# A scan and a gated feed-forward block on one core: unit 1's running states added by VectorE, in a new instruction order

## The chip, the cores and the metric

The kernel runs on one core of a Trainium2 chip. TensorE multiplies, VectorE, ScalarE and GpSimd work on elements, and SyncE's queue issues most transfers. In the profile they are PE (and PEld for its weight loads), DVE, ACT, POOL and SP. The metric is the device time of one execution in microseconds (us); less is better.

## The reference, cut to what matters

```python
# B, H, S, D = 4, 8, 768, 48
mag = sqrt(a_re**2 + a_im**2)
scale = minimum(mag, 0.999) / (mag + 1e-6)
for t in range(S):                       # per batch and head, S_re and S_im are D x D
    S_re, S_im = ar*S_re - ai*S_im + outer(k[t], v[t]), ar*S_im + ai*S_re
    y[t] = q[t] @ S_re                   # ar, ai: a_re, a_im times scale, by row of the state
x = y as (B*S, H*D)                      # 3072 x 384
h = x @ w_in                             # 384 x 2048
g = h * tanh(softplus(h))
out = g @ w_out                          # 2048 x 384
```

The decay of the state is a complex number a row. Written with its size and its angle, the scan becomes products of chunks: with cumulated logarithms of the sizes and cumulated angles, q and k are scaled and turned, and within a chunk y is a masked product of q and k with v, plus q times the state of the chunk before.

## The kernel before, in words

The 3072 tokens are cut into 12 units of 256 (three a batch), and each unit into two chunks, a and b, of 128. For each unit there are three stages.

- **Elementwise.** VectorE and ScalarE make the cumulated sizes and angles and scale q and k. Units 0 and 1 let TensorE add up (lines 404 to 414); later units use VectorE's scans (L486, L501). Relays (L552, DMAs `T<-X` and `T<-QK`, six a chunk) bring the heads into the form that TensorE reads.
- **Attention.** Per chunk TensorE transposes k (`kn`, L608, copied out at L613), multiplies k by q (`am`, L620, masked by VectorE at L627), forms y in `ypsum` (`y`, L638: new part `am` times v, old part q times the old state) and the chunk's contribution to the state (`pd`, L651). VectorE then makes the new state `S` (`S add`).
- **Feed-forward.** Eight blocks p0 to p7: products with w_in (`mm1`, L746), on ScalarE and VectorE the gate (exponential, cap L815, square, logarithm, inverse, gate L759), the split of the result in two halves of fewer bits (`gh` L765, `gl` L771), and the products with w_out (`mm2`, L783). For unit 0 the blocks are q0 to q3 by chunk, in full precision, without the split.

During units 0 and 1 the sixteen pieces of the weights, which come as 64-bit integers, are put together (`low` L279, `shift` L283, `join` L287, `carry` L291) and split in halves (`high` L309, `rest` L314). So the first 110 us or so hold the elementwise work of three units, attention of two, and all the work on the weights.

The state has two forms. With pe the decay of a chunk (column C of T), the first form (`held`) has TensorE put the old state into PSUM by a product with the identity (`hold`, L668), add the chunk's products to it there, and VectorE multiply the sum by pe as it reads it out (L660). The second has VectorE add the old state to the products as it reads them out (L662), and then multiply all by pe in a further instruction (`S fade`, L673, VectorE or GpSimd). `held = u < HELD and not first` picks the form: before, chunks u0b, u1a and u1b are held.

```python
    if first or held:
        pe = T()[:, sl, 0, C].unsqueeze(2).broadcast_to([2 * D, 4, D])
        e.tensor_tensor(d["S"][:, sl, :], d["pd", g], pe, ALU.mult)
    else:
        e.tensor_tensor(d["S"][:, sl, :], d["pd", g], old["S"][:, sl, :], ALU.add)
```

TensorE also has 40 `spin` steps of two products that nobody reads (`junk`, L844), which can stand anywhere between its first steps.

The order is written out: the code above makes a list of steps, and the table `ORDER` gives the sequence in which they are issued, with a letter where a step goes to another engine than its first choice (V VectorE, A ScalarE, G GpSimd, T TensorE, S SyncE). Each engine and each queue works through its steps strictly in that sequence and waits in front of a step whose inputs or buffers are not ready.

Of the kernel before, what the change touches and what calls it, by code (L numbers as in the profile page):

```python
# [44 lines left out]
HELD = 2  # L45
# [8 lines left out]
72 0 1 73 127 3 74 2 75 128 7V 5 8 76 10V 4 9 11 77 6 12 192 78 13 202 197 14 79 24V 80 27V 81 82 25 83 169V 15 19 28  # L54
26 132V 84 16 166V 85 133 22 17 86 167 23 87 31 170 88 32 135V 18 134 34 33 29 137 89 21 136 90 20 91 42 47 46G 45 92
35 48 30 49 93 43 36 44 194 50 193 53 52 94 139 39 95 54 195 96 55 97 40 51 98 37 196V 99 38 100 56A 60 207 101 62A
140 562 102 204 57 563 103 203V 104 199 105 41 200 106 61A 138 107 58 64 108 142 109 59 205 112 66 116 67A 68 113 118
65A 117 70 71A 114 206V 123 69 198 110 119 217 141 120 124 115V 121 201V 125 430 63 143 209 212 126 567 208V 210 144
122 146 186 211V 145 130 168 153 570V 147A 185 173 171 149 148 568 184 151 111 218V 187 174 155 154 571G 360A 129 175
150V 160 152 156 222 157 432 219 569 158 220 356 163 573 161 164 214 159 221V 273 172 189 357 215 188 213 272 191 162  # L60
176 216V 361A 190 358 177 359 227 274 165 363 178 575 275 365 367 276 364 223 224 282 366 572 181A 368 277 225 283 369
576 232 182 179 370 226V 278 292 131 180 229 237 284 279 293 376A 371 183 230 280 374 228 578 574 281 285 231V 372
375A 286 303 378 242 373 287 233V 386 234 388 362 583 302 235 387 382 389 390 288 236V 294 392 434 289 247 383 295 304
312 584 296 385 238 239 379 290 391 381A 384 393 297 380 291 240 442 743 305 243 395 377 244 577 241V 394 298 245 252
306 397 744 400 307 246V 398 446 299 401 257 248 579 322 396 399 308 402 249 403 448 405 580 313 748 404 250 406 323
314 581 251V 407 582 315 262 309 409 316 564 585 408 594A 317 565 300 593 586 324 253 254 301 436 410 431 318 411 263
255 412 258 325 264 414 326 256V 415 587A 417 265 450 267 418 413 332 266V 327 421 259 440 420 433 310 328 566 588 452
423 333 422 438 319 260 343 334 329 589 335 320 592 321 590 428V 595 435 336 311 591 596 426 424 330 337 429 597 603
342 602 598 338 331 425 344 604 427 268 269 601 339 463 749 747 345 609 270 346 462 607 751 261V 605 475 347 933 271V
444 599 340 752 348 608 606 754 474 756 932 349 757 341 437 458 419 350 464 456V 476 439 351 416 465 759 466 610 441  # L70
352 612 487 353 613 611V 354 443 750 614 355 600 477 467 753G 445 486 745 468 746 478 616 758 479 615 469 621 617 488
618 755 470 622 447 619 623 449 480 626 489 624 471 499 760 490 498 940 481 491 451 511 500 625 492 510 764 620 501
628 493 502 482A 494 522 761 503 512 472 454 513 523 763 453 504 627 473 937 505 630 762 629 455 524 631 514 483 535
515 525 765 526 766 534 516 495 767A 517 484 527 768 632 485 528 774 636 506 536 459 496 633 771 769 634 518 507 497
772 635 537 529 508 519 530A 509 773 775A 770 546 639 641 640 460 777 547 637 538 520 548 531 521 784 539 532 938 549
787 642 533 540 638 785 941G 550 541 778 643 551 457 786 939 644 779 542A 790 655 552 543 780 645 942 783 544 788 461
944 545 789 553 782 945 656 943 781 554 1123 668 555 953 646 791 657 954 793 946 556 955 792 794V 647 956 557 648 658
667 957 558 649 559 795 560 1124 650 659 561 1128V 797 947 796 669 679 798 651A 948 660 802 670 776 949 671 800 935
661 799 934 803 1129 804 958 936 806 1131 662 680 950 1130 691 681 672 807V 692 673 805 682 952 674 808 810 809 652
951 801V 812 683 811 653 693 813 663A 1133 684 814 965A 963 675A 815 685 961 817 816V 964A 960 819 664 654 959 686 823  # L80
694 825 665 962 967 824 1135 822 703 695 676 968 704 974 973 716 971 705 696 706 666 975 1144 1132 697 978 828 677 698
707 977 1136 966 1145 1305 715 970 830 687 976 728 717 972 708 718 727 688 969 709 1134 980 826 678 719 979 699 720
831 1304 689 710 721 1146 829 1137 690 700 729 818 1125 827 701 1138 1147 1126 711A 702 722 1139 832 820 1148 821 833
712 730 981 1312V 834 713 1140 723A 982 845 724 731 1141 983 985 984 732 714 733 1142 734 725 1309 1149 844 1143 735
835 856 736 836 1155G 986 1150 726 1154 1151V 1153 737 1152 987 1157 846 857 738 988 837 1158 838 992 739 994 741 993
740 839 1127 997 989 742 995 858 1156 847 1310 998V 990 996 848 1313G 999 991V 1163 1001 1000 840 1162 849 1003 1161
1311 841 1160 869 850 1002 1494 1314 842 851 1316 868 1004 1317 1325 1005 859 1006 1315 860 1008 1326 1164 861 1010
862 880 852A 1007V 1167 870 881 1493 871 1169 1011 872 863 843 1165 873 853 1013 882 892 874 1166 883 1318 875 1014
854 884 1327 1170 1319 893 1159 1320 864A 1016 1328 855 894 865 1015 885 1321 1168 905 886 895 1017 904 1009 896 1018
887 897 866 876 1307 906 1019V 877 898 1306 867 1501 1020 899 1498 878 907 888 908 1021V 1171 1022 1499 1173 900 917  # L90
1322 909 1172 916 910 1174V 879 918 919 1024 1329 920 1500 1502 1175 1324 1177 1176 1506 889 1023 921 911 1323 890
1012 922 1504 1335G 912A 891 1178 1025 1336G 1036 1026 1503 1180 1332V 1334 1179 1182 1330 901 1184 913 1035 923 1183
924A 902 1185 1331 1186G 903 914 925 1333 1685 1338 915 1027 1505 926 1028 1345 1339 927 1341 1514 1047 1037 1346 928V
1507 1038 1343 1515 1048 1039 1348 1029 1181V 1351 1187 1040 929 930 1030 1189 1308 1508 1340 1509 1060 1516 1049 1188
1344 1041 1190 931 1191 1342 1050 1337 1517 1192 1042 1059 1193 1031 1518 1051 1194 1032 1071 1052 1347 1510 1043A
1350 1033 1053 1349 1061 1072 1196 1062 1054 1063 1684 1034 1197 1064 1195 1073 1352 1065 1495 1354 1074 1083 1044
1055A 1496 1075 1056 1045 1689 1066 1692V 1076 1084 1202V 1511 1077 1096 1200 1690 1095 1198V 1085 1078 1067A 1199
1046 1201 1097 1519 1108 1079A 1086 1098 1087 1203 1057 1512 1068 1099 1058 1100 1069 1353 1080 1101 1513 1070 1088
1526G 1107 1355 1089 1356 1691 1090 1524 1358 1091A 1521 1081 1102 1204 1357 1109 1092 1205 1103 1082 1110 1359 1111
# [108 lines left out]
def tile_kernel(ctx, tc, q, k, v, are, aim, are_t, aim_t, w_in, w_out, out):  # L208
# [373 lines left out]
    def attention(u, between):  # L582
# [488 lines left out]
```

## Time and profile before

| | |
|---|---|
| runs | 589.53, 592.84, 592.3 us; median 592.3 |
| the profiled execution, its own time | 591.61 us |
| its span, first to last instruction | 589.8 us |
| granted TensorE clock, mean | 0.998 |
| ACT table loads in the profile | 44 and a first one, 1283 ns each |

A row of the windows view gives, for a stretch of the span, the time that each engine was busy in it, with the number of instructions in brackets, the granted clock and the share of the DMA engines. A row of the groups view gives line, engine, operation, tiles, shape and count, then the busy time of all and the mean of one in ns, and the idle time ahead of them. A row of the timeline gives the start, the length, the engine and the instructions that were merged, with the idle time before it in square brackets. Matmuls overlap, so the time of several is best read from the start of one row to the start of the next. A float32 product that counts as one instruction in the order stands as two in the profile; transposes and products in fp32r stand as one.

### The profile page before, as it was taken

How to read it: one execution, taken by the hardware profiler on the slowest of the kernel's cores; microseconds unless marked ns; L12 is line 12 of the kernel's file. 1: busy time of each engine (PE TensorE's matmuls, PEld its weight loads, DVE VectorE, ACT ScalarE, POOL GpSimd, SP SyncE). 2: the span in 40 equal slices, each digit the busy share in tenths (PEclk: the TensorE clock that was granted, in tenths of full speed). 3: DMA queues.
4: the chain of work that ended last, by engine and by line, in shares of the span. 5: the costliest groups of instructions: out<-in, count | busy, mean ns of one | idle time of the engine just before them, and what ended most of it. 6: DMA issues, size and time to landing. Idle time of an engine off the chain costs nothing.

```text
span 589.8 us, 11893 instructions
## 1 busy us (share of the span) xinstructions
PE 580.6 (98%) x4654; PEld 550.0 (93%) x4654; DVE 469.6 (80%) x830; ACT 474.4 (80%) x762; POOL 21.4 (4%) x36
## 2 busy tenths in 40 slices
PE   8999999999999999999999999999999999999996
PEld 4688887899999999999999999999999999999996
DVE  6999999999999889886779978878777855455453
ACT  7899999899997999689988859776974966555582
POOL 1010000101000100000001001001000000000000
PEclk9999999999999999999999999999999999999999
DMA  8788975403626352270171081261064043001000
GB/s 290 250 260 251 300 217 148 137 12 93 181 75 180 84 149 66 75 222 1 43 209 46 10 233 55 69 202 55 11 180 108 1 121 87 26 13 28 28 1 32
DMA packets 57248, 67.07 MB, mean 114 GB/s; under 512 B 4832, under 2 KB 50272, under 8 KB 57184
## 3 DMA queue, kind: packets, MB, share of 16 engines
q1 hardware_dynamic: 56464, 65.57, 37.8%
q8 instruction: 39, 0.64, 0.5%
q10 hardware_dynamic: 720, 0.66, 0.4%
q14 instruction: 25, 0.20, 0.1%
HBM read 37.75 MB, written 4.72 MB: 72 GB/s over the span
## 4 chain that ended last, share of the span: by engine, by line
PE 83%; DVE 5%; DMA 5%; ACT 4%; issue 1%; SPq 1%; POOL 0%; DVEq 0%; ACTq 0%; POOLq 0%
PE po L783 32%; PE ph L746 31%; PE pa L620 6%; PE ypsum L638 6%; PE pd L651 4%; PE pkn L608 2%; DMA words<-w_in 2%; PE junk L844 2%; DMA T<-X 1%; DMA x<-y 1%; DVE w L291 1%; DVE w L287 1%; ACT e L172 1%; DMA T<-QK 1%; ACT L170 1%
## 5 line engine op out<-in xcount | busy, mean ns | idle before, releaser
L172 ACT ACTIVATE e<-e 128x512 f32<-128x512 f32 x192 | 118.2, 627 | 31.8 <-DVE e L815 30.5
L746 PE MATMUL ph<-xH,wh 128*128 128x256 f32 x462 | 132.9, 288 | 0.0
L746 PE MATMUL ph<-xL,wh 128*128 128x256 f32 x462 | 129.7, 281 | 0.0
L746 PE MATMUL ph<-xH,wl 128*128 128x256 f32 x462 | 129.6, 280 | 0.0
L783 PE MATMUL po<-wh,gh 128*128 128x384 f32 x308 | 106.0, 344 | 0.0
L783 PE MATMUL po<-wh,gl 128*128 128x384 f32 x308 | 104.3, 338 | 0.0
L783 PE MATMUL po<-wl,gh 128*128 128x384 f32 x308 | 104.2, 338 | 0.0
L746 PEld LDWEIGHTS ph<-xH,wh 128*128 128x128 f32 x462 | 87.0, 188 | 0.9 <-issue 0.4
L746 PEld LDWEIGHTS ph<-xL,wh 128*128 128x128 f32 x462 | 87.0, 188 | 0.3
L746 PEld LDWEIGHTS ph<-xH,wl 128*128 128x128 f32 x462 | 87.0, 188 | 0.0
L759 DVE SCALAR_TENSOR_TENSOR g<-e,ph 128x512 f32<-128x512 f32 x96 | 65.3, 681 | 27.1 <-ACT e L172 26.7
L172 ACT ACTIVATE e<-ph 128x512 f32<-128x512 f32 x96 | 56.5, 590 | 36.9 <-PE ph L746 31.8
L771 DVE TENSOR_TENSOR gl<-g,gh 128x512 fp32r<-128x512 f32 x88 | 60.0, 684 | 17.0 <-ACT gh L765 10.5
L172 ACT ACTIVATE e<-e,fifth 128x512 f32<-128x512 f32 x96 | 68.8, 719 | 1.3
L815 DVE TENSOR_SCALAR e<-e 128x512 f32<-128x512 f32 x96 | 40.4, 424 | 26.6 <-ACT e L172 26.4
L783 PEld LDWEIGHTS po<-wh,gh 128*128 128x128 f32 x308 | 57.9, 188 | 0.2 <-issue 0.2
L783 PEld LDWEIGHTS po<-wh,gl 128*128 128x128 f32 x308 | 57.9, 188 | 0.1
L783 PEld LDWEIGHTS po<-wl,gh 128*128 128x128 f32 x308 | 57.8, 188 | 0.0
L170 ACT ACT_TABLE_LOAD x44 | 56.5, 1283 | 0.7
L620 PE MATMUL pa<-T 96*128 96x128 f32 x384 | 49.1, 277 | 0.9 <-DVE am L627 0.8
L620 PEld LDWEIGHTS pa<-T 96*128 96x128 f32 x384 | 46.0, 191 | 1.7 <-DVE am L627 1.0
L627 DVE TENSOR_TENSOR am<-pa,cmask 128x512 f32<-128x512 f32 x48 | 32.4, 684 | 5.3 <-PE pa L620 5.3
(135 smaller groups left out, 1053.1 us busy)
## 6 DMA issues: line engine op xcount, KB each, us to landing
T<-QK SPq DMA_DIRECT2D x70, 129.0 KB, 3.2
T<-X SPq DMA_DIRECT2D x69, 129.0 KB, 3.2
words<-w_in SPq DMA_DIRECT2D x8, 768.0 KB, 6.6
words<-w_out SPq DMA_DIRECT2D x8, 768.0 KB, 5.3
QK<-k SPq DMA_DIRECT2D x12, 384.0 KB, 4.5
QK<-q SPq DMA_DIRECT2D x12, 384.0 KB, 4.6
V<-v SPq DMA_DIRECT2D x12, 384.0 KB, 4.5
R<-a_re SPq DMA_DIRECT2D x12, 384.0 KB, 4.2
```

Source lines behind the costliest of these rows:

```text
L170: self.nc.scalar.preload_act_table_set(need)
L172: return self.nc.scalar.activation(out, in_, func, **kw)
L608: e.transpose(d["pkn", g][:, i, :], T()[:, 4 * g + i, 1, :C], ident)
L620: e.matmul(d["pa", g][:, i, :], T()[:, 4 * g + i, 1, :C], T()[:, 4 * g + i, 0, :C], start=True, stop=True)
L627: e.tensor_tensor(d["am", g], d["pa", g], cmask.unsqueeze(1).broadcast_to([P, 4, C]), ALU.mult)
L638: e.matmul(ypsum[64 * par:64 * par + D, i, :], lhs, rhs, start=m == 0, stop=first or m == 1)
L651: e.matmul(d["pd", g][:, i, :], d["kn"][:, h, :], st["V"][:, c, h * D:(h + 1) * D], start=not held, stop=not held or i == 3)
L746: e.matmul(ph[k][:, slot(k, j, a), :], win(x, j, kt, a), st[y][:, kt, cols(k)], start=n == 0, stop=n + 1 == len(todo))
L759: e.scalar_tensor_tensor(g_[k], e_[k], 2.5, ph[k], ALU.subtract, ALU.mult)
L771: e.tensor_tensor(gs[k][1], g_[k], gs[k][0].bitcast(F32), ALU.subtract)
L783: e.matmul(po[t], x[:, slot(k, j, a), 0 if halved else t * P:C if halved else (t + 1) * P], wout(y, j, a), start=j == 0 and a == 0 and n == 0,
L815: op("V", f"{n} cap", lambda e, k=k: e.tensor_scalar_min(e_[k], e_[k], math.exp(20.0)))
```

## The change

`HELD` goes from 2 to 1: only u0b is still held. Chunks u1a and u1b lose their two `hold` steps each (L668 in the list before) and get a `S fade` step each; their `S add` steps add the old state instead of multiplying by pe. The table `ORDER` is another one, with the numbers of the steps shifted, other places for most steps, and other engines for some. Its text is one line shorter, so that every line of the code stands one line higher afterwards (L668 becomes L667).

```diff
-HELD = 2
+HELD = 1
 ...
 ORDER = [(int(x.rstrip("VAGTS")), x.lstrip("0123456789")) for x in """
-72 0 1 73 127 3 74 2 75 128 7V 5 8 76 10V 4 9 11 77 6 12 192 78 13 202 197 14 79 24V 80 27V 81 82 25 83 169V 15 19 28
+72 0 1 73 2 3 74 128 75 127 7V 5 8 76 4 10V 9 77 11 192 202 14 24V 78 197 25 6 15 79 26 17 80 16 12 81 27V 13 82 135V
 ...
```

TensorE at chunk u1a, before: the end of `y`, the two holds, the state's products, then a block of unit 0's feed-forward and the transposes of u1b.

```order
L638 MATMUL ypsum<-T,S 48x128 x2
L638 MATMUL ypsum<-am,V 48x128 x2
L668 MATMUL pd<-S,identity 96x192 x2
L651 MATMUL pd<-V,kn 96x48 x8
L746 MATMUL ph<-x,w 128x128 x6
L608 MATMUL pkn<-identity,T 128x96 x8
```

The same place afterwards.

```order
L637 MATMUL ypsum<-T,S 48x128 x2
L637 MATMUL ypsum<-am,V 48x128 x2
L650 MATMUL pd<-V,kn 96x48 x8
L745 MATMUL ph<-x,w 128x128 x6
L782 MATMUL po<-w,g 128x384 x2
L745 MATMUL ph<-x,w 128x128 x6
L607 MATMUL pkn<-identity,T 128x96 x8
```

The row of holds is gone, and two products of a feed-forward block with w_out and one more group with w_in now stand between the state's products and the next transposes.

VectorE where it makes the state of u1a, before (`w` and `words` are the weights, `e` and `g` the gate of unit 0, `R` the sizes of unit 2):

```order
L759 SCALAR_TENSOR_TENSOR g<-e,ph 128x512
L485 SCALAR_TENSOR_TENSOR R<-X 128x768
L660 TENSOR_TENSOR S<-pd,T 96x192 x2
L283 TENSOR_SCALAR w<-words 128x768
L486 SCALAR_TENSOR_TENSOR R<-rmask,R 128x768
L287 SCALAR_TENSOR_TENSOR w<-words,w 128x768
```

The same place afterwards.

```order
L661 TENSOR_TENSOR S<-pd,S 96x192
L758 SCALAR_TENSOR_TENSOR g<-e,ph 128x512
L286 SCALAR_TENSOR_TENSOR w<-words,w 128x768
L661 TENSOR_TENSOR S<-pd,S 96x192
L290 ISA w<-words,w 128x1536
L672 TENSOR_TENSOR S<-S,T 96x384
L282 TENSOR_SCALAR w<-words 128x768
```

The two sums now read the old state, stand apart, and are followed, one step later, by the multiplication by pe.

Of the 40 spin steps, 38 stand ahead of the first transposes of u0a before, and 34 afterwards; the other 2 and 6 stand between there and `am` of u1a.

Other moves between engines, by count of steps, before and afterwards: `carry` of the weights on GpSimd 0 and 2 (pieces 2 and 11), on VectorE 16 and 14; `low` on VectorE 4 and 1, on ScalarE 12 and 15; `S fade` on GpSimd 3 and 5 (both of unit 1's are on VectorE); `gh` on ScalarE 43 and 51, on VectorE 45 and 37. ScalarE's table loads in the body go from 44 to 46; the two more are reached by the end of unit 2's feed-forward. The six relays of u0a stand on SyncE's queue afterwards, a relay from `QK` first; before, one of the six was on ScalarE's queue, and the queue of SyncE began with two from `X`.

More of the change, by code (lines that the diff above doesn't have):

```diff
@@ L58 @@
[L58 to L87, printed above, removed]
@@ new lines @@
+317 259 421 585A 256V 291 420 326 563 586 318 332 418 327 264 263 419 588V 319 267 310 328 265 587 311 329 266V 342
+258 260 589 438V 333 261V 426 590 330 334 422 456 320 591 335 594 336 424 321 337 593 338 601 595 343 268 599 448 600
+331 427 344 597 339 436 425 607 345 340 446 564 423 269 930 346 270 602 461 747 603 433 452 460 604 750 347 598 473
+596 348 271V 462 472 435 748 341 349 463 474 437 350 352 416 754 353 414 475 605 351 464 752 606 476 439 931 465 608
+610 458 751 484 609 417 611 485 441 354 466 355 612 477 743 467 755 744 443 614 468A 613 496 478 445 486 497 756 487
@@ new lines @@
+447 753 619 615 616 757 620 617 479 469 498 621 762 624 488 499 618 449 508 935 758 470 489 763 500 759 471 490 501
+509 480A 622 491 502 623G 626 625 510 503 760 520 764 492A 521 761 511 481 773A 512 628 627 513 493 629 522 765 504A
+451 482 630 936 453 631 483 514 632 766 772A 938 634 533 774 515 633 769 771 494 745 768 495 505 523 532 516A 457 524
+506 517 770 775 525 507 545 782 777 526 544 776 635 534 636 518 639 785 535 637 527 1121 536 519 783 638 537 640 778
+528 454 642 529 781 546 455 784 530 538 937 779 547 539 641 786 548 939 780 549 531 788 941 550 787 540A 653 551 943
@@ new lines @@
+821 696 714 1136 969 1137 819 676 977 705 697 822 706 1131 726 971 707 698 715 967 687 1138 1133 978 725 1139 976 970
+688 828 829 1141 699 708 1124 709 700 710 1123 727 716 826 824V 711 1142 717 728 1310V 729 979 827 1140 981 825 712
+1307V 718 1153G 982V 730 1143 830 719 1144 731 831 720 980 732 721A 983 1145 832 733A 985 722 1146A 734 843 1308 1152
+984 842 1309 986 833 1311 855 834 835 1147 990 844 992 1149V 836 991 1148 723 1312 845 724 993 1151 1150 854 735 1155
+736 1162 995 737 988 1314 738 1157 996 987 994 739 1492 837 846 997 1491 1323 999 1156 998 856 1165 1324 1325 1001
@@ new lines @@
+1043 1194 1064 1053A 1494 1517 1083 1044 1193 1688 1084 1076 1493 1093 1085 1054 1065A 1690V 1350 1086 1352 1520V 1106
+1519 1066 1077 1055 1691 1196V 1521 1094 1056 1095 1067 1198 1096 1087 1199 1068 1097 1088 1078 1105 1089A 1200V 1098
+1518 1090 1079 1107 1201 1197 1099 1693 1080 1100 1203 1108 1523 1522 1109 1202 1689 1214 1351 1204 1524A 1353 1354
+1205 1110 1356 1111 1206 1112 1091 1695 1101 1102 1215 1113A 1355 1696 1092 1692 1207 1357 1694 1103 1114 1104 1208
+1703 1525 1115 1526 1116 1533 1528 1226 1117 1119 1118 1216 1361 1864 1209 1535 1363 1217 1210A 1863 1358 1364 1529
@@ new lines @@
+1362 1359 1211 1527 1365 1704 1367 1538 1366 1227 1218 1368V 1495 1536 1219 1239 1228 1534 1220 1238 1537 1229 1230
+1221 1539 1369 1222 1532 1240 1231 1120 1371 1370 1698 1251 1372 1705 1212 1223 1241 1706 1213 1685 1242 1697 1684
+1360V 1250 1232 1233 1373 1699 1252 1374 1243 1253 1700 1254 1376 1244 1378 1375 1707 1262 1702 1382 1377 1245 1234A
+1384 1263 1708 1255 1531 1256 1275 1381 1379 1264 1257 1383 1701 1224 1265 1686 1235 1266 1530 1225 1710V 1246A 1713
+1712 1709 1274 1287 1389V 1387V 1711 1247 1236 1871V 1276 1714 1385V 1258 1237 1715 1390 1248 1267 1259 1868 1277 1249
@@ new lines @@
+1888 1722 1882 1558 1560 1729 1422 1431 1727 1891V 1413 1890 1423 1728 1889 1559V 1451 1561 1432 1452 1866 1414 2057
+1562 1433 1440 2058 1563 1434 1565 1441 1424 1453 2060V 1564 2059 1442 1454 1567 1443 1435 1455 1569 1566 1464 1456
+1570 1572 1568 1444 1865 1730 1894A 1895A 1732 1457 1575 1463 1445 1573 1446 1425 1867 1458 1574 1465 1436 1447A 1476
+1576V 1466 1426 2061 1437 2065 1459 1448 1467 1438 2062 1468 1577 1449 1469 2063 1580 1450 1470 2066 1896 1460 1475
+1571 1471 1461 1581 1477 1472 1578V 1462 1478 1579 1479 1893 1473 1480 1481 1582 1731V 2067 1482 1594 2064 1483 1484
@@ new lines @@
+1474 1897 1607 1892 1733 1734 2073 1904 1485 1735 1486 2074 1595 2068 2069 1583 1736 1584 1596 1585 1741 1597 1586
+1738 1737 1587 2075 1742 1739 1487V 1489 1588 1488 1743 1906 1740 1598 1746 1899 1744 1589 1599 1898 1606 2070 1590A
+1900 1905 1618 1608 1600 1745 1748 1609 1909 1601 1619 1901 2076 1490 1631 1591 1907 1620 1602A 1902 1621 1592 1747
+2077A 2244 1749 1903 1610 1630 1908 1622 1611 2243 1750 1612 1751 1623 1613 1624 1911 1752V 1632 1913 1593 1603 1614A
+1755 1625 1753 1643 1633 1756 1615 1634 1754 1642 2078 1626A 1635 1910 1654 1644 1636 1645 1655 2072 1637 1646 2248V
@@ new lines @@
+2054 1604 1656 2055 1761 1657 1605 2249 2251 1616 1627 1638A 1762 1666 1647 2252 2071 1617 1658 1757 1667 1659 1648
+1628 1759 1649 2250 1758 1629 2084A 1760 1668 1650 1660 1764 1661 1639 1763 1662A 1912V 2081 2079 1640 1669 2253 1670
+1914 1641 1651 1671 2083 1672 1776 2256 1652 1673 2254 1775 2085 1663 2257 1915 2082 2259 1917 1916 1653 1918 1674
+2255 1664 1675 2080 1922 1765 1788 1923 1665 1766 2087 1767 1676 2258 1677 1768 2264 2086 2090 2260 1777 1924 2088
+1678 1778 1926 1925 1920 2094 1927 1919 1779 1928 1769 1930 1680 1770 2095 1787 1929V 1681 1931 2100 1932 1921V 1679
@@ new lines @@
+1789 2097 1780 1800 1933 2324 2099 1771 1935 2265 2096 1772 2098 1934 1790 1937 1791 1936V 1781 1939 2261 1792 1799
+1944 1793 1945 1782 1773 2092 1801 1811 2089 1802 1794 2091 1803 1774 1783 1942 1804 1940 1784 1943 1805 1812 2093
+1785 2056 1813 2245 2262 1814 1824 2246 1806 1795A 2263 1823 1796 1786 1825 2274A 1815 1826 1836 2266 1816 1807A 1797
+1817 1827 1835 1818 1828 1946V 1947 1798 1837 1950V 1951 1819A 1808 1847 1829 1938 1948V 1949 1848 1838 1830 1809 2267
+1831A 1849 2101 2103 1850 2102 1953 1820 2104 1839 2276 2105 1840 1841 2107 2106 1851 1952 2108 2268 2112 1941 2114
@@ new lines @@
+2113 2110 2115 2269 2109 1842 2270 2117 2273 2275A 1852 2119 1810 1965 1843 1954 2120V 1853 1821 1955 2118 1854 1964
+2116 1832 1822 2271V 2277 2272 1833 1966 1834 1855 2278 1844 2121 1856 1967 2123 2122 1968 2284 1976 2111 1845 2124
+2290 1846 2286 2247 1857 2328 2279 1858 2285 2126 2288 1859V 1861 1956 1860 2125 1957 1862 2281 2128 1958 2287 1969
+1959 2130 2282 1970 1977 1960A 2127 1989 1978 2134 1979 1988 2325 1961 1980 2135 1971 1962 2133 1990 2136 1981 1963
+1991 2283 1972A 2289 1992 2000 1982 2329 2280 1993 2001 1983 2141 1973 2013 2002 2137 2003 1994 2012 1984 2004 1995
@@ new lines @@
+2173 2333 2317 2191 2181 2174 2314 2163A 2192 2316 2164 2315 2182 2153 2183 2184 2154 2193 2165 2194 2195 2203 2185
+2318 2175A 2204 2319 2320V 2196 2176 2322 2166 2186 2197 2205 2198 2215 2206 2321 2207 2216 2208 2227 2187A 2199 2217
+2188 2228 2209 2210 2177 2229 2178 2230 2323 2218 2189 2219 2211 2200 2231 2190 2334 2220 2232 2336 2212 2221 2222
+2201 2223A 2202 2335 2213 2337 2233 2347 2234 2235 2214 2224 2338 2348 2236 2339 2225 2349 2350 2226 2351 2340 2237
+2352 2238 2360 2239 2241V 2341 2240 2359 2242 2342 2343 2372 2361 2353 2362 2371 2344 2363 2354 2345 2373 2346 2374
```

106 lines of the change are left out of this document (40 added, 66 removed).

## Prediction, on record before the result was known

> **What bounds the kernel now.** I read the page first, then the busy time by stretches, then the timeline of TensorE and VectorE in the first 110 us. The page, span and busy times:
>
> ```profile
> span 589.8 us, 11893 instructions
> ...
> PE 580.6 (98%) x4654; PEld 550.0 (93%) x4654; DVE 469.6 (80%) x830; ACT 474.4 (80%) x762; POOL 21.4 (4%) x36
> ```
>
> The busy time by stretches; the columns behind the stretch are its length, then PE, PEld, DVE, ACT and POOL with their counts, the granted clock, and the transfers:
>
> ```profile
> 16.00:55.00 39.00, 38.58 (x323) 32.02 (x322) 38.23 (x65) 37.00 (x65) 1.95 (x1) 1.00 0.76 235
> 55.00:105.00 50.00, 49.60 (x367) 40.78 (x366) 48.70 (x79) 47.82 (x76) 0.00 (x0) 1.00 0.77 235
> 105.00:150.00 45.00, 44.32 (x369) 42.97 (x367) 42.84 (x70) 43.40 (x68) 3.85 (x2) 1.00 0.29 81
> 150.00:200.00 50.00, 49.99 (x408) 49.12 (x406) 47.79 (x81) 45.62 (x75) 0.56 (x1) 1.00 0.42 118
> 200.00:250.00 50.00, 50.00 (x441) 49.02 (x440) 43.91 (x78) 42.41 (x67) 3.33 (x4) 1.00 0.39 107
> 250.00:500.00 250.00, 249.22 (x2064) 245.12 (x2064) 194.29 (x350) 198.29 (x316) 7.75 (x5) 1.00 0.35 98
> 500.00:584.00 84.00, 84.00 (x632) 83.08 (x631) 42.96 (x85) 46.56 (x79) 0.85 (x1) 1.00 0.06 17
> 584.00:589.80 5.80, 0.62 (x4) 0.30 (x2) 0.18 (x1) 0.49 (x1) 0.00 (x0) 0.80 0.21 73
> ```
>
> TensorE hardly waits from 16 to 584 us: 565.7 of 568.0 us are busy, so 2.3 us of plain idle time is all that another order could close there, and the 5.8 us at the end are the last output and its store, which the change leaves alone. From 16 to 105 us VectorE is as full as TensorE: 86.9 of 89.0 us. After 200 us it has 6 us to spare in 50, and from 250 us a fifth of its time. So TensorE's own work sets the time after 200 us, and ahead of that two engines run full side by side, and ScalarE, 84.8 of 89.0, is nearly a third. What is taken off one of them ahead of 105 us comes out at the end only if the other lets it.
>
> **The change part by part: what TensorE loses.** TensorE's timeline at the states of u1a and u1b (start, length, instructions):
>
> ```profile
> 67.69 0.89 PE L668 MATMUL pd<-S,identity 96*96 96x192 f32 x4
> 68.41 1.48 PE L651 MATMUL pd<-V,kn 128*96 128x48 f32 x16
> ...
> 80.87 0.57 PE L668 MATMUL pd<-S,identity 96*96 96x192 f32 x2
> 81.27 0.80 PE L651 MATMUL pd<-V,kn 128*96 128x48 f32 x8
> 81.91 0.53 PE L668 MATMUL pd<-S,identity 96*96 96x192 f32 x2
> 82.28 0.80 PE L651 MATMUL pd<-V,kn 128*96 128x48 f32 x8
> ```
>
> From each start to the next row the holds take 0.72, 0.40 and 0.37 us: 1.49 us that TensorE no longer works. They stand with no gap in a full queue. If nothing else limited, the end would come 1.49 us sooner.
>
> **What VectorE gains and loses.** The groups that price it (busy time, then the mean of one in ns):
>
> ```profile
> L673 DVE TENSOR_TENSOR S<-S,T 96x384 f32<-96x384 f32 x10 | 7.6, 765 | 0.0
> L291 DVE CUSTOM_DVE_ANT_0 w<-words,w 128x1536 uint16<-128x1536 uint16 x16 | 15.1, 950 | 0.4
> L279 DVE TENSOR_SCALAR words<-words 128x768 int32<-128x768 uint32 x4 | 2.2, 554 | 0.6 <-DMA words<-w_in 0.6
> L613 DVE COPY kn<-pkn 128x384 f32<-128x384 f32 x13 | 7.1, 544 | 0.3 <-PE pkn L608 0.3
> L452 DVE SCALAR_TENSOR_TENSOR X<-R 128x768 f32<-128x768 f32 x3 | 2.8, 949 | 0.0
> L465 DVE TENSOR_TENSOR X<-X 128x768 f32<-128x768 f32 x6 | 5.7, 950 | 0.0
> L516 DVE TENSOR_SCALAR R<-I 128x768 uint32<-128x768 uint32 x6 | 3.3, 551 | 0.0
> L309 DVE CAST wh<-w 128x768 fp32r<-128x768 f32 x1 | 0.5, 549 | 0.0
> L314 DVE TENSOR_TENSOR wl<-w,wh 128x768 fp32r<-128x768 f32 x14 | 13.6, 974 | 0.0
> L468 DVE SCALAR_TENSOR_TENSOR X<-R,X 128x768 f32<-128x768 f32 x10 | 9.5, 952 | 0.0
> L712 DVE CAST xH<-x 128x256 fp32r<-128x256 f32 x16 | 4.5, 286 | 1.9 <-DMA x<-y 1.9
> L527 DVE COPY QK<-X 128x12 f32<-128x12 f32 x4 | 0.7, 170 | 0.0
> L465 POOL TENSOR_TENSOR X<-X 128x768 f32<-128x768 f32 x4 | 7.4, 1846 | 104.2 <-ACT X L172 104.2
> ```
>
> I take the new order of VectorE up to the last gate of unit 0 (the eighth L759), the last thing of unit 0 that TensorE asks of it, and set it against the old one. Gone from in front of it: four `low` (4 x 0.554 = 2.22), two `carry`, now on GpSimd (2 x 0.950 = 1.90), one copy of kn (0.54), one cast of x (0.29), the test of unit 3 (0.95): 5.90 us. New in front of it: the fade of u1a (0.77), one `low` (0.55), two copies of kn (1.09), the first two steps of unit 2 that were ScalarE's and GpSimd's (0.95 and 0.95), an `abs` (0.55), one `high` (0.55), one `rest` (0.97), three copies of ends (3 x 0.17 = 0.51, the longer form as an upper price): 6.89 us. VectorE has 0.99 us more to do there, or about 0.7 if each further instruction overlaps its neighbour by 0.1 us, as the rows below start before the one ahead has ended. The sums at `S add` keep their number and shape: nothing. The fade itself is 0.77 of it; the second one, u1b's, comes after the gate.
>
> A carry in whole numbers on GpSimd isn't in the trace. The nearest rows are its own sum of the same size, 1.85 us, and VectorE's carry, 0.95, so I take 1.85. Piece 2 is joined as VectorE's 29th step and first used by unit 0's feed-forward, which stands behind all of its attention; piece 11 is first used by a block of unit 1. That hides both, and if it didn't the product would wait for the 0.9 us between the two rows.
>
> **Where the two meet.** VectorE's gate and TensorE's three groups of four products around it:
>
> ```profile
> 101.66 0.68 DVE L759 SCALAR_TENSOR_TENSOR g<-e,ph 128x512 f32<-128x512 f32 x1
> ...
> ```
>
> ```profile
> 101.74 4.03 PE L783 MATMUL po<-w,g 128*128 128x384 f32 x12
> ```
>
> The second and third group use that gate: the second begins at 101.74 + 4.03/3 = 103.08, the gate ends at 102.34. The margin is 0.74 us. Afterwards TensorE would be there at 103.08 - 1.49 = 101.59, and the gate ends at 103.0 to 103.3. So TensorE waits some 1.4 to 1.7 us, and goes on 0.0 to 0.25 us later than before: the holds' time turns into a wait for VectorE. This rests on VectorE being full from 16 us on in the new order as well, since the same steps start it. Its 2.1 us of idle time from 16 to 105 us are the most it could win.
>
> **The start.** The spin rows and SyncE's relays of u0a, with the first transposes:
>
> ```profile
> 1.71 8.03 PE L844 MATMUL junk<-cmask 128*128 128x512 bf16 x24 [1.71 <-POOL cmask L226]
> ...
> 18.57 7.07 PE L844 MATMUL junk<-cmask 128*128 128x512 bf16 x32
> 25.48 0.50 PE L608 MATMUL pkn<-identity,T 96*128 96x96 f32 x4
> ```
>
> ```profile
> 17.67 1.95 SPq L552 DMA_DIRECT2D T<-X  x2
> 19.80 1.20 SPq L552 DMA_DIRECT2D T<-QK  x2
> 21.04 0.61 SPq L552 DMA_DIRECT2D T<-X  x1
> ```
>
> Four spin steps fewer ahead of the transposes are 8 x 0.221 = 1.77 us less, but the transposes need the relays. All six now follow the later of the two turns, whose relays began at 19.80 at the latest; a pair of them took 1.20 us to issue, so six end at 23.4 at the latest, where the last ended at 21.65 before, 3.83 us ahead of the transposes. So the transposes come between 25.48 - 1.77 = 23.7 (if the relays are there by then) and 23.4 + 3.8 = 27.2 us. I take 26, nearer to the upper end since the issues are certain. That is 0.5 us late, and VectorE has work of its own ahead of its first step on them. The four spin steps come back between u0b's `am` and u1a's, where VectorE sets the pace; if it doesn't, they cost 1.77 us.
>
> **The sum.** To the end of unit 0's blocks: -1.49 by TensorE, turned into +0.1 by the wait for VectorE. From there to 200 us VectorE is 90.6 of 95 us full, and counted to the last split of unit 1's blocks its lead in work stays under 1 us: +0.2. The tail: 0. That is +0.3 on the profiled execution's own 591.6 us (589.8 of span and 1.8 around it), 591.9; the median of the runs, 589.5 to 592.8, is 592.3, 0.7 above that execution. I say 592.0. A measurement here can tell about 0.5%, 3.0 us, from no change: the bounds are 589.3 and 595.3.
>
> **The rivals.** *TensorE's saving comes through.* VectorE closes its own idle time, or the gate comes earlier, since two carries left it and the relays of u0a end sooner: 591.6 - 1.5 = 590.1, and with the 2.3 us of TensorE's idle time closed, 587.8. For it: 2.1 us of gaps on VectorE. Against it: its work grew.
>
> *Slower: unit 2's splits come late.* From 105 to 200 us ScalarE is busy 89.0 of 95.0 us, and the new order gives it two more table loads by the end of unit 2's blocks, and eight more `gh` in all.
>
> ```profile
> L170 ACT ACT_TABLE_LOAD x44 | 56.5, 1283 | 0.7
> ```
>
> Two loads are 2.57 us. TensorE's `mm2` waits for `gl`, which waits for `gh`, which stands behind them on ScalarE. With VectorE's 1.0 that is 3.6 us, and the time 591.6 + 3.6 = 595.2, or to 597 if the spin steps' 1.77 come on top. It decides if ScalarE's idle time there, 6.0 us, isn't where the loads fall. To this rival belongs that GpSimd's two carries, 1.85 us each, hold up VectorE beside them: at most 3.7 us, 595.3, with 0.02 of its chance. What the trace shows of two such neighbours:
>
> ```profile
> 36.18 1.95 POOL L465 TENSOR_TENSOR X<-X 128x768 f32<-128x768 f32 x1 [21.12 <-ACT X L172]
> ...
> ```
>
> ```profile
> 36.18 0.55 DVE L279 TENSOR_SCALAR words<-words 128x768 int32<-128x768 uint32 x1
> ```
>
> VectorE's `low` began together with a sum of GpSimd and took 0.55 us, the mean of its group. The Trainium skill ("GPSIMD Engine Reference", section 8, Key points) says that GpSimd shares its SBUF interfaces with VectorE and contends with VectorE's instructions in a 2-port mode or with two inputs there. By that rule the carries would cost VectorE time; in this pair of rows it shows no cost on VectorE's side.
>
> *A long early wait halves TensorE's clock.* The first 24 spin products took 335 ns each, and the 32 later ones 221: TensorE begins slowly after idling. The wait for the transposes is at most 27.2 - 23.7 = 3.5 us by the sums above. If that is long enough to bring the slow start back, the products after it go at up to twice the time for as long as it lasts, here less than the 8.0 us of that row: up to 4 us more, and 1.7 for the late transposes (27.2 - 25.5), 597.3. Against it: the value that I take is 2.3 us of wait. The Trainium skill ("TensorE: Matmul & The Clock Gate", Part 1: The HAM clock gate) puts the idle window that throttles at about 3.4 us; by that figure only the upper end of this wait would do it.
>
> **How the numbers follow.** Forecast, 591 to 593.5: 0.52. The saving comes through: 0.25, of which 0.10 below 589.3. Splits late: 0.18, of which 0.13 over 595.3. Slow clock: 0.05, all over. So faster 0.10, slower 0.18, the same 0.72. The range goes from 589.0, the saving with half the gaps closed, to 596.0, the late splits with the spread of the runs: about one in five is left out.
>
> **What would show it.** Right: no L667 product at u1a or u1b; TensorE idle or spread out by 1.4 to 1.7 us ahead of the last products of unit 0, put down to VectorE; those products within 0.5 us of 103 us. The sum of TensorE's idle time from 16 to 584 us would be 3 to 5 us. Wrong: the last products of unit 0 at 101.6 us and a span near 588 (the first rival), or an idle TensorE between 130 and 200 us with ScalarE named as the one it waits for (the second), or spin rows of over 300 ns after 25 us (the third).

## The result, and the profile after

The changed kernel takes 596.17 us (median; 594.85 to 597.41), against 590.83 us for the kernel before on the same chip (589.53 to 592.84). The ratio is 1.0085, 95% interval 1.0067 to 1.0103: 4.0 to 6.1 us slower. The prediction, 592.0 us within 589 to 596, put 0.18 on slower. The profiled execution took 596.17 us itself, with 4.7 us more span than the one before. Span and busy times:

```profile
span 594.5 us, 11891 instructions
...
PE 581.4 (98%) x4646; PEld 550.1 (93%) x4646; DVE 469.7 (79%) x830; ACT 480.5 (81%) x769; POOL 18.2 (3%) x33
```

The stretches that answer to those shown of before (length, PE, PEld, DVE, ACT, POOL, granted clock, transfers):

```profile
16.00:55.00 39.00, 34.20 (x280) 28.91 (x279) 34.73 (x60) 33.33 (x57) 2.53 (x1) 0.96 0.71 209
55.00:105.00 50.00, 48.48 (x363) 38.98 (x362) 47.35 (x78) 47.82 (x75) 2.58 (x2) 1.00 0.73 215
...
150.00:200.00 50.00, 49.90 (x410) 48.45 (x409) 49.20 (x90) 47.55 (x72) 0.95 (x1) 1.00 0.43 117
```

The loss is in the first row. From 16 to 55 us TensorE was busy 38.58 of 39 us before and is 34.20 now, 4.4 us less. That this is nearly the whole difference is in part chance: 1.49 us of it are a wait for ScalarE at 19.60, ahead of spin products that nobody reads, and slow products, shown below, count as busy. VectorE went from 38.23 to 34.73 and ScalarE from 37.00 to 33.33, so no engine is busier there; all three wait. The mean clock is 0.96, where it was 1.00. From 150 to 200 us TensorE differs by 0.1 us.

Who waits for whom? First VectorE from 32 to 36 us:

```profile
32.33 0.96 DVE L451 SCALAR_TENSOR_TENSOR X<-R 128x768 f32<-128x768 f32 x1 [2.75 <-DMA R<-a_re]
...
33.29 0.35 DVE L659 TENSOR_TENSOR S<-pd,T 96x192 f32<-96x192 f32 x1
...
34.90 0.35 DVE L659 TENSOR_TENSOR S<-pd,T 96x192 f32<-96x192 f32 x1
```

L451 is the first step of unit 2's sizes. It stood on ScalarE before; the new order puts it on VectorE, ahead of the two additions that make the first state (L659, chunk u0a). It waits 2.75 us for the load of unit 2's R, and the additions wait behind it, though everything they need is there. TensorE at the same time:

```profile
30.36 0.88 PE L650 MATMUL pd<-V,kn 128*96 128x48 f32 x8
33.79 1.67 PE L403 MATMUL psum<-less,X 128*128 128x128 f32 x12 [2.55 <-DVE S L659]
35.30 0.80 PE L408 MATMUL psum<-turn,I 128*128 128x128 f32 x2
...
38.02 0.76 PE L607 MATMUL pkn<-identity,T 96*128 96x96 f32 x4
```

Its next step takes one of the two PSUM banks that the additions read, so TensorE stands for 2.55 us. The rows behind that are slow: from L408 at 35.30 to L607 at 38.02 are 2.72 us for six pairs that took 1.35 us before. The granted clock in stretches of 2 us shows why:

```profile
34.00:36.00 2.00, 2.00 (x15) 1.87 (x15) 2.00 (x4) 1.86 (x4) 0.00 (x0) 0.79 0.98 353
36.00:38.00 2.00, 2.00 (x11) 2.00 (x11) 1.86 (x4) 1.26 (x4) 0.00 (x0) 0.50 1.00 361
38.00:40.00 2.00, 2.00 (x19) 1.97 (x18) 1.46 (x3) 1.73 (x4) 0.00 (x0) 0.86 1.01 390
```

Chunk u0b begins on TensorE at 38.02 us. Before, its first row was

```profile
34.09 1.08 PE L620 MATMUL pa<-T 96*128 96x128 f32 x8
```

so TensorE is 3.9 us behind here. Why R comes so late is on SyncE's queue and ScalarE's:

```profile
23.21 0.60 SPq L551 DMA_DIRECT2D T<-X  x1
23.86 0.59 SPq L369 DMA_DIRECT2D I<-a_im  x1
28.45 0.33 SPq L369 DMA_DIRECT2D R<-a_re  x1
28.91 0.56 SPq L551 DMA_DIRECT2D T<-X  x1
29.58 0.73 SPq L551 DMA_DIRECT2D T<-QK  x1
30.40 0.54 SPq L272 DMA_DIRECT2D words<-w_out  x1
30.99 0.55 SPq L551 DMA_DIRECT2D T<-X  x1
```

```profile
24.43 0.66 ACTq L551 DMA_DIRECT2D T<-X  x1
```

The queue's waits put a number and a name on the hole between 23.86 and 28.45:

```profile
SPq L369 <- DMA T<-X: 4.0, 1, 4.0
```

As the program is built, the DMAs of both queues take turns on eight completion semaphores (101 to 108 in the trace), and a DMA waits at the head of its queue until the one before it on its semaphore has landed. The load of R got its turn behind a relay of u0b that ScalarE's queue issued at 24.43; both have semaphore 107. That relay landed 4.0 us after its issue, at 28.4, and R was issued at 28.45. So it waited 4.0 us for a transfer with which it has nothing to do, and what stood behind it waited too: SyncE's three relays of u0b (28.91, 29.58, 30.99) and a weight piece (30.40). SyncE's queue before:

```profile
21.80 0.47 SPq L273 DMA_DIRECT2D words<-w_out  x1
22.32 0.45 SPq L370 DMA_DIRECT2D R<-a_re  x1
...
29.97 1.21 SPq L552 DMA_DIRECT2D T<-QK  x2
```

There the weight piece (`w3`) and both loads, 22.3 and 22.8 us, held up nothing. But the last of SyncE's relays of u0b was issued near 30.6, hardly earlier than now. What differs is when it landed. The last field is the time from issue to landing, of the last relay before and then now:

```profile
T<-QK SPq DMA_DIRECT2D x1, 129.0 KB, 2.4
```

```profile
T<-X SPq DMA_DIRECT2D x1, 129.0 KB, 6.5
```

It landed near 33.0 before and at 37.5 now. The new order puts the load of `w3`, 768 KB, directly ahead of it, and the DMA engines were fully busy until then (a share of 1.00 from 30.40 to 37.50 us).

Two things therefore came late at once: VectorE's row with R, and u0b's last relay. Was it these, or the new arithmetic, or something else of the new order?

### The profile page after: what moved, and what is told of

It is laid out like the page before. It is cut to its first block, busy times and chain, and to the rows that moved or that the text cites. A ratio compares the mean times of both kernels' runs of the same rounds, so it can differ in the third digit from the quotient of the medians.

```text
span 594.5 us, 11891 instructions
## 1 busy us (share of the span) xinstructions
PE 581.4 (98%) x4646; PEld 550.1 (93%) x4646; DVE 469.7 (79%) x830; ACT 480.5 (81%) x769; POOL 18.2 (3%) x33
## 4 chain that ended last, share of the span: by engine, by line
PE 67%; ACT 17%; DVE 4%; DMA 4%; issue 2%; SPq 0%; ACTq 0%; DVEq 0%
PE po L782 26%; PE ph L745 25%; ACT e L171 6%; PE pa L619 5%; PE ypsum L637 5%; ACT X L171 4%; PE pd L650 3%; ACT L169 3%; DMA words<-w_out 2%; DMA T<-X 2%; PE pkn L607 2%; ACT words L171 1%; ACT R L171 1%; ACT wh L308 1%; ACT gh L764 1%
## 5 line engine op out<-in xcount | busy, mean ns | idle before, releaser
L764 ACT CAST gh<-g 128x512 fp32r<-128x512 f32 x51 | 31.1, 611 | 10.2 <-DVE g L758 10.1
```

What stands on the lines that cost most here:

```text
L764: (e.copy if e is nc.scalar else e.tensor_copy)(gs[k][0], g_[k])
```

## The experiments

Each kernel was compared with the kernel before on the same chip, and ratios are to that. Edits are shown as steps of the order by name, with the engine; in the kernel before and in those whose text is as long as its, every line number is one higher than in the changed kernel. The first two take away VectorE's wait for R, in two ways; the next two part the arithmetic from the order.

**Unit 2's size row behind the additions.** The theory at first was the row on VectorE alone.

```diff
 (changed kernel, VectorE)
-u2 size r
 u0b count, u0a S add0, u1b size, w1 carry, u0a S add1
+u2 size r
```

> The changed kernel with one VectorE row moved: unit 2's first size row (it needs the load of unit 2's R, which lands at 32.3 us) goes behind both additions of the states of unit 0's first chunk, not ahead of them; the ScalarE row that reads it goes with it. Theory (this wait holds two PSUM banks, TensorE idles 2.55 us for them and then runs at half clock for some 4 us, where one product of 1.34 us took 2.72): the additions fall near 30 us, the wait of 2.55 us and about 1.9 us of slow rows go, 596.2 - 4.4 = 591.8 us, between 590.8 and 592.8. Rival 'arithmetic' (the fades on VectorE or the missing holds cost the time): no change, 595.5 to 597. Rival 'late unit 2' (unit 2's own chain comes too late): unit 2 gets about 1 us later still, 596 to 598.

Measured: 597.21 us, 1.0087 (1.006 to 1.0113). No gain: the theory of one wait falls. The additions no longer wait, but TensorE stops at the transposes of u0b and of u1a, which read relays:

```profile
35.99 0.52 PE L607 MATMUL pkn<-identity,T 96*128 96x96 f32 x4 [2.76 <-issue]
...
60.99 0.85 PE L607 MATMUL pkn<-identity,T 96*128 96x96 f32 x8 [2.15 <-DMA T<-X]
```

For the first the profile names no releaser ("issue"). SyncE's queue still held the relays of u0b behind R and, the last of them, behind `w3`. That one was issued at 30.80 us and landed 5.1 us later, at 35.9, just ahead of that row:

```profile
26.71 0.33 SPq L369 DMA_DIRECT2D R<-a_re  x1
...
30.80 0.55 SPq L551 DMA_DIRECT2D T<-X  x1
```

**R's load ahead of I's.**

```diff
 (changed kernel, SyncE)
-I2 load, R2 load
+R2 load, I2 load
```

> The changed kernel with the loads of unit 2's R and I exchanged on SyncE's queue, all else as it stands. Theory: R is issued at 23.9 instead of 28.4 us and lands near 28 instead of 32.3, so VectorE's row that waits for it starts when VectorE is free (29.6), the states' additions come about 2.7 us earlier and TensorE's wait of 2.55 us for their PSUM banks shrinks below 0.5: 591.5 to 593.5. If the place of that row counts and not the load, 595.5 to 597. Rival 'arithmetic': no change, 595.5 to 597.

Measured: 597.14 us, 1.0089 (1.006 to 1.0118). Now I's load is the one that waits, and the relays stay behind it; the last lands 6.7 us after its issue at 29.92. So TensorE waits 3.33 us at the transposes of u0b:

```profile
27.53 0.33 SPq L369 DMA_DIRECT2D I<-a_im  x1
...
36.74 0.87 PE L607 MATMUL pkn<-identity,T 96*128 96x96 f32 x4 [3.33 <-issue]
```

**The old order with the new arithmetic.**

```diff
 (kernel before)
-HELD = 2
+HELD = 1
-u1a hold0, u1a hold1, u1b hold0, u1b hold1   TensorE
+u1a S fade, u1b S fade                       VectorE, each behind its two S add
```

> The kernel before in its old order, with the change of arithmetic alone: the four products with the identity are left out, and unit 1's states are added up and faded by VectorE, each fade right behind its chunk's two additions. Theory (the new order costs, not the arithmetic): 590.8 less at most 1.5 us for the holds, plus at most 0.7 us for VectorE's fades, 589.3 to 591.5. Rival 'arithmetic': most of the loss of 5.3 us is here, 594 to 596.

Measured: 592.0 us, 1.0013 (0.9991 to 1.0034). That is 0.5 us above the range expected. The arithmetic costs nothing that can be told from zero; it doesn't save its 1.5 us either. TensorE's waits from 16 to 584 us suggest where they went:

```profile
PE ph L746 <- DVE g L759: 1.0, 2, 0.5
...
PE ph L746 <- DVE w L291: 0.4, 1, 0.4
```

These 1.4 us of waits for VectorE's gates and weights don't occur in the kernel before.

**The new order with the old arithmetic.**

```diff
 (changed kernel)
-HELD = 1
+HELD = 2
+u1a hold0, u1a hold1, u1b hold0, u1b hold1   TensorE, each ahead of its pd
-u1a S fade, u1b S fade
```

> The changed kernel's new order with the old arithmetic: the four products with the identity are back, each right ahead of the products that add to it, and the two fades are gone. Theory (the new order costs): TensorE gets back 1.5 us of products, 596.2 to 598, about 597.5. Rival 'arithmetic': 590.5 to 592.5.

Measured: 596.84 us, 1.0089 (1.0056 to 1.0123). The whole loss is there without the new arithmetic.

So it is the order, and not VectorE's wait for R alone. The next theory was two waits side by side, each long enough to hide what taking away the other brings.

**R's load behind the relays, with the row at its place and with the row behind.**

```diff
 (changed kernel, SyncE)
-R2 load
 u0b relay sin2, u0b relay cos0, w3 load, u0b relay sin1
+R2 load
```

> The changed kernel with the load of unit 2's R alone put behind the relays of unit 0's second chunk; unit 2's first size row stays ahead of the states' additions. New theory (two waits side by side): the relays come early, but R lands near 34 us, so VectorE's wait and with it TensorE's for the two PSUM banks is 1 to 2 us longer than in the changed kernel: 596 to 598. If SyncE's queue alone is the cause: 591 to 593.5.

```diff
 (the same, VectorE)
-u2 size r
 u0b count, u0a S add0, u1b size, w1 carry, u0a S add1
+u2 size r
```

> The changed kernel with both put back: unit 2's first size row behind the additions of unit 0's states (as in the first experiment), and the load of unit 2's R behind the relays of unit 0's second chunk on SyncE's queue. New theory (two waits side by side: VectorE's row that waits for R, and SyncE's queue, where the load of R waits 3.6 to 4.4 us for a DMA of another queue and holds back three relays of unit 0's second chunk, which TensorE needs at 33 us; taking away one leaves the other): with both gone 591 to 593.5. Rival (neither; weights come late and DMA is full from 28 to 44 us): 595 to 597.

Measured: load alone 601.34 us, 1.0171 (1.0145 to 1.0197); with the size row behind the additions as well 599.0 us, 1.0137 (1.0111 to 1.0163). Both are worse than the changed kernel. The first goes in the expected direction, further than expected, with TensorE's wait for the additions at 6.5 us:

```profile
PE psum L403 <- DVE S L659: 6.5, 1, 6.5
```

The second missed its expectation, but doesn't test the theory: the turns on the semaphores shifted by one, and now the relay behind I's load had the wait, 3.5 us, while R landed so late among the weights that VectorE waited 5.5 us for it. The last relay of u0b, again behind `w3`, landed 6.9 us after its issue at 28.98:

```profile
SPq L551 <- DMA T<-X: 3.5, 1, 3.5
```

```profile
DVE X L451 <- DMA R<-a_re: 5.5, 1, 5.5
```

**Both loads early.** A cleaner way to take both waits away is to issue the loads when SyncE's queue and the DMA engines have nothing to do.

```diff
 (changed kernel, SyncE)
 V0 load
+R2 load, I2 load
 u0a relay cos1, sin1, cos0, sin2, cos2, sin0
-I2 load, R2 load
```

> The changed kernel with the two loads of unit 2's R and I issued ahead of the first relay of unit 0 on SyncE's queue, where the DMA engines have nothing to do, not behind unit 0's relays. So neither VectorE's row for R nor SyncE's queue waits for them any longer. Theory (these two loads, at their place between the relays of unit 0's two chunks, cost the time): 591.5 to 594. Rival (the order of the first 45 us costs in other ways too, or later stages do): 595 to 597.

Measured: 592.9 us, 1.0026 (1.0008 to 1.0044). Of 0.85%, 0.59% or 3.5 us are back by moving two loads. VectorE has no wait for R in the profile, and the last relay of u0b, issued at 29.17, lands at 34.9, not 37.5.

```profile
8.72 0.43 SPq L369 DMA_DIRECT2D R<-a_re  x1
```

**Both loads early, and the size row behind the additions.**

```diff
 (run above, VectorE)
-u2 size r
 u0b count, u0a S add0, u1b size, w1 carry, u0a S add1
+u2 size r
```

> The changed kernel with the loads of unit 2's R and I ahead of all relays (as before: 592.9 us) and unit 2's first size row behind the additions of unit 0's states as well. Theory (the row costs by its wait for R alone, and R is there): within 0.7 us of 592.9, 592.2 to 593.6. Rival (the row's own 0.96 us ahead of the additions, or its place, costs part of the 2 us that are left): 591 to 592.

Measured: 592.37 us, 1.0027 (1.001 to 1.0044), the same as without the row's move. With R there, the row's place costs nothing that can be told.

**Each wait by itself, put into the kernel before.** If either is enough, each must cost time in the old order.

```diff
 (kernel before, SyncE)
-u0b relay sin1, u0b relay cos1, u0b relay cos0
 w5 load
+u0b relay sin1, u0b relay cos1, u0b relay cos0
```

> The kernel before, its arithmetic and all its order kept but for one thing: SyncE's three relays of unit 0's second chunk stand behind the load of the sixth weight piece, so that they are issued near 32 instead of 26 to 31 us. New theory: TensorE, which reads that chunk at 34.1 us, waits 2 to 3 us for it and may run some 4 us at half clock behind that: 593 to 596. If such a delay is hidden by slack: 590.5 to 591.5.

```diff
 (kernel before)
-R2 load                   SyncE
 u0b relay sin1, u0b relay cos1
+R2 load                   SyncE
+u2 size r                 VectorE
 u0a S add0
-u2 size r                 ScalarE
```

> The kernel before, arithmetic and order kept but for two rows: the load of unit 2's R stands behind a relay of unit 0's second chunk (issued near 30 instead of 22.3 us), and unit 2's first size row stands on VectorE ahead of the additions of unit 0's states, not on ScalarE. Theory (VectorE's wait for R is by itself enough): VectorE waits from 29.6 to about 35 us, TensorE waits some 4 us for the two PSUM banks and may run at half clock behind that: 594 to 598. Rival (it costs only together with the rest of the new order): 590.5 to 592.

Measured: late relays 594.93 us, 1.0065 (1.004 to 1.009); size row ahead with a late R 597.25 us, 1.0108 (1.0081 to 1.0135). Each alone makes a loss, 3.9 and 6.4 us, in an order that is otherwise the old one. In the first the three relays were issued at 29.54, 30.19 and 30.80 us. The last is thus hardly later than in the kernel before, so what this run delays is less the issue than the landing: a weight load stands ahead of the relays, and they landed some 5 us after their issue, where the three took 3.7, 2.3 and 2.4 us before. TensorE went on when the last had landed (ScalarE's row, named as the releaser, had long been done). The view of tile T gives the landing, the timeline the wait:

```profile
DMA to landing us min/median/max: 4.8/4.9/5.0
```

```profile
35.84 1.13 PE L620 MATMUL pa<-T 96*128 96x128 f32 x8 [1.96 <-ACT X L172]
```

This profile is of the fastest of the run's six executions, 592.07 us, so it shows the wait but not the whole loss. In the second, VectorE waits for R, TensorE for VectorE's copy of kn behind it, and the clock is halved; the wait is longer than the changed kernel's, 4.39 against 2.55 us, and so is the loss:

```profile
32.86 0.96 DVE L452 SCALAR_TENSOR_TENSOR X<-R 128x768 f32<-128x768 f32 x1 [3.52 <-DMA R<-a_re]
```

```profile
34.70 1.48 PE L651 MATMUL pd<-V,kn 128*96 128x48 f32 x8 [4.39 <-DVE kn L613]
```

```profile
36.00:38.00 2.00, 2.00 (x11) 2.00 (x11) 1.74 (x4) 0.00 (x0) 0.00 (x0) 0.50 0.81 144
```

**Where in the order.** The steps are issued from one list of 2432. Two kernels join the head of one order to the tail of the other, with the new arithmetic in both; a third takes a shorter head of the old order, to about 31 us.

```diff
-ORDER = new
+ORDER = old[:234], then all others as in new      (old start)
+ORDER = new[:234], then all others as in old      (new start)
+ORDER = old[:160], then all others as in new      (short old start)
```

> The new arithmetic, with the first 234 of 2432 steps (to about 45 us) in the old order and all others in the new order. Theory (the loss of 5.3 us is made in the first 45 us): 590.5 to 593. Rival (it is made later): 595 to 597.

> The new arithmetic, with the first 234 of 2432 steps (to about 45 us) in the new order and all others in the old order. Theory (the loss is made in the first 45 us): 594.5 to 597.5. Rival (it is made later): 590.5 to 592.5.

> The new arithmetic, with the first 160 of 2432 steps (to about 31 us, with the loads of unit 2's R and I at 22 to 23 us and the relays of unit 0 at their old places) in the old order and all others in the new order; unit 2's first size row is then VectorE's first row of the new order, ahead of the second addition of unit 0's states. Theory (what counts is where the loads and relays stand on SyncE's queue, before 31 us): 590.5 to 593. Rival (the row's place on VectorE or the order from 31 to 45 us counts): 594 to 597.

Measured: old start 591.77 us, 1.0013 (0.9997 to 1.003); new start 597.67 us, 1.0109 (1.0082 to 1.0137). The first 45 us of the order make the loss, and the other 550 us of it none that can be told. The same windows, of the old start and then of the new start:

```profile
16.00:55.00 39.00, 38.31 (x328) 32.27 (x327) 38.16 (x65) 36.95 (x65) 2.14 (x2) 1.00 0.81 250
```

```profile
16.00:55.00 39.00, 35.44 (x290) 29.99 (x289) 34.40 (x59) 33.35 (x55) 2.52 (x1) 0.96 0.75 227
```

Short old start: 593.46 us, 1.0029 (1.0009 to 1.0049), between the two expectations. Loads and relays as of old up to 31 us take back most of it, though unit 2's size row stands on VectorE ahead of an addition there. In its profile, of the slowest of twelve executions (595.08 us), the transposes of u1a wait, 2.92 us, for relays that the order behind 31 us issues:

```profile
58.94 1.35 PE L608 MATMUL pkn<-identity,T 96*128 96x96 f32 x7 [2.92 <-DMA T<-X]
```

**The half clock.** Five spin steps keep TensorE busy in its wait of 2.55 us.

```diff
 (changed kernel, TensorE)
-SPINS, SPIN = 40, 2
+SPINS, SPIN = 45, 2
 u0a pd1
+spin, spin, spin, spin, spin
 u1a mag sum
```

> The changed kernel with five more spin steps (of about 0.43 us each, on TensorE alone, results unused), put into TensorE's wait ahead of unit 1's first sum of magnitudes. The wait stays as long, but TensorE isn't idle in it. If the half clock behind the wait (rows of 1.34 us took 2.72) has its own price: about 1.8 us less than the changed kernel, 593.5 to 595. If the price is the late data alone: 595.5 to 597.

Measured: 596.52 us, 1.009 (1.0064 to 1.0115): no gain that can be told. In the profile the wait is filled (the products begin at 32.82), and the pairs behind it take 0.22 us each, full speed:

```profile
30.37 2.32 PE L844 MATMUL junk<-cmask 128*128 128x512 bf16 x10
32.82 1.58 PE L404 MATMUL psum<-less,X 128*128 128x128 f32 x12
...
34.88 0.39 PE L409 MATMUL psum<-turn,I 128*128 128x128 f32 x2
35.10 0.39 PE L414 MATMUL psum<-ncar,identity 128*128 128x128 f32 x2
```

So the half clock is real in the profiled execution, but the 1.4 us that it adds to those rows can't be shown in the time. The landings say why this run could hardly show them. In the changed kernel u0b's last relay landed at 37.5 and TensorE reached u0b at 38.02, so without the slow rows TensorE would have stood for that relay, and at most some 0.4 us were to be won. Here the relay, issued at 30.56, landed 5.4 us later, and u0b began 0.1 us behind it, at 36.05. What the half clock costs where nothing else is late stays open.

**The fades on GpSimd.** The old order and the new arithmetic, looking for the saving of 1.5 us.

```diff
 (third kernel)
-u1a S fade, u1b S fade   VectorE
+u1a S fade, u1b S fade   GpSimd
```

> The old order with the new arithmetic (as in the third experiment, 592.0 us), but the two fades on GpSimd in place of VectorE. If the 1.5 us that the missing holds free on TensorE are lost to VectorE's two fades in unit 0's stages (TensorE then waits 0.3 to 0.5 us a time for VectorE's rows): 590 to 591.3. If GpSimd's fade, longer than VectorE's, comes too late for the next chunk or slows VectorE beside it: 592 to 593.5.

Measured: 592.39 us, 1.0017 (0.9999 to 1.0034), no better. Without the fades on VectorE TensorE still waits 1.0 us for its gates, as in the third experiment, so it isn't the fades that make those waits; GpSimd's fade of u1a took 3.61 us. No version tried is faster than the kernel before.

## Why the prediction was wrong, point by point

- **TensorE loses four holds, 1.49 us: right.** No L667 stands at u1a or u1b.
- **The saving turns into a wait for VectorE: right in sum, wrong in place.** The old order with the new arithmetic measures +0.8 us (-0.5 to +2.0) where the prediction's sum had +0.3, and TensorE's waits there grew by 1.4 us for gates and weights. In the changed kernel the place named, the last gate of unit 0, has no wait: the group that uses the gate begins at 107.80 + 4.04/3 = 109.15, the gate ends at 108.73. It comes 6.1 us later than before, not within 0.5 us of 103.

```profile
107.80 4.04 PE L782 MATMUL po<-w,g 128*128 128x384 f32 x12
```

```profile
108.05 0.68 DVE L758 SCALAR_TENSOR_TENSOR g<-e,ph 128x512 f32<-128x512 f32 x1
```

- **Prices.** The fade of u1a took 0.54 us, not 0.77: the group's mean of ten hid a median of 0.55 and a longest of 1.92. GpSimd's carry in whole numbers took 2.45 us in the mean of two, not 1.85. Beside the first of them VectorE's own carry, at 26.47, took its usual 0.95 us, so it shows no cost on VectorE.
- **The start: transposes at 26 us: right in time, with luck**; they began at 26.06. The six relays were issued until 23.8 us, later than the 23.4 "at the latest", and the transposes followed 2.3 us behind, not 3.8; the two misses cancel.
- **The step that failed: "VectorE being full from 16 us on in the new order as well, since the same steps start it".** VectorE idles 4.27 us from 16 to 55, against 0.77 before, and 2.75 of it is the wait for R. TensorE's idle time from 16 to 584 us is 7.1 us, where 3 to 5 were forecast. The prediction knew that two steps of unit 2 came to VectorE, and priced them as work, 0.95 us each. It didn't ask what the first of them waits for, nor what is queued behind it. The row needs a load; the load stands behind the relays of u0a on SyncE's queue and waits there for a semaphore; and three relays of u0b stand behind the load, the last of them behind a weight piece as well. That one question, where each load sits in SyncE's queue and who stands behind it, was asked only of the six relays of u0a.
- **What it cost.** Of the 0.85% (5.0 us), the head of the order makes 0.72% (4.3 us; changed kernel against old start), and the place of the two loads 0.59% (3.5 us; against loads early). The 0.13% of the arithmetic can't be told from zero, nor what is left between the early loads and the old start.
- **The rivals.** *TensorE's saving comes through* didn't happen in any kernel tried. *Slower by unit 2's late splits* had a time near the true one, 595.2 us, for a reason that isn't there: from 150 to 200 us TensorE idles 0.10 us. *A long early wait halves the clock* had the right effect, 0.05 of the chance, and the wrong wait: the one for the first transposes stayed at 0.76 us, and the clock fell 8 us later. The range, to 596.0, ended just short: a wait between these two places wasn't among its cases. That it missed by only 0.2 us is luck: the sum started from a profiled execution of 591.6 us and a median of three runs of 592.3, where seven gave 590.83. As a change, +0.3 us was forecast, and +5.3 measured.

Still open: why the early loads and the short old start keep some 1.6 us (each between 0.5 and 2.9). In their profiles TensorE waits 1.0 to 2.9 us at u1a's transposes near 59 us, against 0.4 before; that wasn't tried by itself. Two of these profiles are of the slowest execution of their run, but early loads with the size row behind, profiled at 592.43 us, shows 1.08 us there. Both kernels with early loads also wait 0.7 us at u0b's transposes, which begin 0.1 us after the last relay has landed, the one behind `w3`. Moving `w3` alone behind that relay wasn't tried, so how much of the loss is its own isn't shown.

## What to carry to other kernels

Price a step that moves to another engine by the work it adds and also by the last input it waits for: in a queue that runs strictly in order, its wait becomes the wait of everything behind it, and one load's turn on a shared semaphore can hold up relays that have nothing to do with it. Look at when a transfer lands, not only at when it is issued: a small relay behind a weight piece took 6.5 us here, and 2.4 without one just ahead. If taking away a wait brings nothing, look for a second one of the same length beside it before giving up the cause; putting each alone into the good kernel shows it. Loads whose buffers are free belong where the queue is idle, ahead of the first DMA that waits for data.

## What the runs showed of the hardware that was not expected

TensorE's clock fell to half after waits shorter than the 3.5 us of the prediction's third rival. After 2.15 us (the first experiment, row at 60.99) the granted clock was

```profile
62.00:64.00 2.00, 2.00 (x13) 1.66 (x13) 2.00 (x4) 2.00 (x5) 0.00 (x0) 0.62 0.85 237
64.00:66.00 2.00, 2.00 (x10) 1.91 (x9) 1.11 (x1) 2.00 (x3) 0.00 (x0) 0.53 0.87 194
```

and after 2.55 us in the changed kernel 0.50. Counted as half rate, these two rows make 1.52 + 1.88 us and the changed kernel's three 0.84 + 2.00 + 0.56 us: 3.4 us in both. Yet 2.76 us, in the same first experiment at 35.99, left it at full speed:

```profile
36.00:38.00 2.00, 2.00 (x18) 1.88 (x19) 1.83 (x3) 1.08 (x3) 0.00 (x0) 1.00 1.00 385
```

So no single length of wait decides it here. The Trainium skill ("TensorE: Matmul & The Clock Gate", Part 1: The HAM clock gate) has the clock halved after at least one idle window of about 3.4 us; these rows show the half rate, but after 2.15 and 2.55 us.
